# Four weights' low parts on GpSimd, and the first Fourier stage of the second tokens in half-sized steps

## The chip, the cores and the metric

The kernel runs on one core of one Trainium2 chip. The metric is device time in microseconds (us) for one execution. The core's engines work side by side, each through its own queue in order: TensorE (PE, with its weight loads as PEld), VectorE (DVE), ScalarE (ACT), GpSimd (POOL), and SyncE (SP), which here only issues DMAs. ScalarE and GpSimd issue DMAs too. An engine waits where an instruction needs something that another engine or a DMA has not delivered, and whatever stands behind it in that queue waits with it.

## The reference

Both branches start from the layer-normalized input, and their sum is added to the input:

```python
xn = _layernorm(x)                      # x: 1 x 2048 x 448
# A: a state-space filter, as a convolution by FFT of length 4096
K = 2.0 * einsum("dn,dnl->dl", C, exp(A * dt * pos)).real
y = irfft(rfft(xn) * rfft(K))[:2048] + xn * D_skip
# B: a gated unit with 1792 inner features
h = sigmoid(xn @ w_gate) * (xn @ w_up)
out = x + y + h @ w_down
```

## The kernel before

The kernel is written in two generators, `conv()` for branch A and `glu()` for branch B. A driver at the end of the kernel steps them alternately, by estimated cost, so that the program has their instructions interleaved. The compiler's scheduler then fixes one order for each engine from the order of the program, from priorities, and from a model of when each instruction could start; instructions inside `hp(HP)` count as if they stood 300 places earlier. On the chip this order does not change. Tiles come from pools: a tile's tag has a fixed number of buffers (`bufs`), and a new tile waits until an older one of that tag is done with.

**Branch B.** The 2048 tokens are worked on in two halves of 1024, each in two groups `t` of 512. The 1792 features are 14 blocks `f` of 128, in five groups (3, 3, 3, 3, 2 blocks). A weight is kept as the sum of a rounded high part and a low part, so that each product is three matmuls: high by high, low by high, high by low. In the first half of the tokens, for each `f` (lines 741 to 764): the raw weights are loaded into `wraw` (one buffer, by SyncE), ScalarE rounds them to `wh` (line 748), VectorE subtracts to get `wl` (line 752; for the very first weight line 750), and for some `f` both are stored for the second half. In the second half some weights are loaded raw again and split on GpSimd (lines 757 to 759). `gate(w, xs, ...)` for a pair (f, t) then issues two groups of 11 matmuls (line 698), each into one PSUM bank of the tag `gu` (four buffers); ScalarE takes the tanh of the first bank (L706), VectorE multiplies by the second into `hf` (L709), ScalarE rounds it to `hh` (L714) and VectorE makes `hl` (L716). Both have six buffers. After all blocks of a group, the down matmuls go into `po` (line 811, also tag `gu`), and VectorE adds them to `acc` (L816). The down weights' low parts `dl` are made on GpSimd (L775).

**Branch A.** `prep` turns the filter's parameters into tables, in long runs of VectorE operations with single ScalarE steps (lines 336 to 417); its low parts are subtractions on GpSimd (L393). It runs while the first two groups of branch B do. `kgen` then makes the filter in 56 chunks: GpSimd the magnitudes (L503), PE the phases into `tr` (L526), ScalarE the sines `S` (L535 to L538), VectorE the products `Et` and `Ft` (L589 to L591), PE the sums `ko` (L603). `spectra` multiplies the spectra and transforms back, in the last quarter.

**The first Fourier stage** of the input (`x_first_stage`, line 281) makes four pieces g of each pair of token blocks, each by two matmuls into one bank. For blocks 0 to 7 `x_spec` does it. For blocks 8 to 15 it is put into the last feature group of the first half (`cross`, f = 12 and 13), whose gates run in the order (12, 0), (13, 0), (12, 1), (13, 1). There each pair of blocks b = 8, 10, 12, 14 goes through four steps: `pair_load` brings its tokens into two tiles with the tags `hh` and `hl`; `pair_norm` normalizes them; `pair_turn` transposes them for branch B's second half; and `pair_first` does the Fourier stage: it takes four `gu` banks, issues eight matmuls into them (sixteen rows of the profile, which shows each of these float32 matmuls as two), and copies each bank to an `x1` tile (two pieces in the single `wraw` buffer, two in the two `rd` buffers), from which ScalarE's queue issues two DMAs each. Three tables say where the steps stand: `mid[n]` between the two matmul groups of the n-th gate, `end[n]` behind that gate, `downs[t, b]` behind the down matmuls of group t and block b.

Of the kernel before, what the change touches and what calls it, by code (L numbers as in the profile page):

```python
# [32 lines left out]
WS = 4.5  # L33
WP = 5
WX = 2
HELD = 12.6
HP = 300
Y0 = (8, 1)
# [92 lines left out]
def s4d_glu_kernel(ctx, tc, io):  # L131
# [142 lines left out]
    def row(b, g):  # L274
        return 32 * (b // 4 % 2) + 8 * g + 4 * (b // 8) + b % 4
# [391 lines left out]
        with hp(HP):  # L667
            x_transpose(xns, xq[-1], 128 * (b % 4))

    def pair_first(b, xns):  # L670

        x1 = pg.tile([128, 2, D], F32, name="x1", tag="wraw", bufs=1)
        pss = [psg.tile([128, 512], F32, name="gu", bufs=4) for _ in range(4)]
        for g in range(4):
            x_first_stage(pss[g][:, :D], xns, g)
        for g in range(4):
            to = x1[:, g] if g < 2 else pg.tile([128, D], F32, name="x1", tag="rd", bufs=RB)
            nc.scalar.copy(to, pss[g][:, :D])
            for i in range(2):
                nc.scalar.dma_start(x1_d[:, row(b + i, g)], to[64 * i : 64 * i + 64])  # L680

    def gate(w, xs, to, between=None, behind=False):
        wh, wl = w
# [35 lines left out]
    def glu():  # L719
        for half in range(2):  # L720
# [4 lines left out]
            for fs_ in ORDER[half]:  # L725
# [8 lines left out]
                if cross:  # L734
                    xts = {b: pair_load(b) for b in range(8, 16, 2)}
                    step = lambda f_, b: f_(b, xts[b])
                    mid = [(pair_norm, 8), None, (pair_first, 8), (pair_first, 10)]
                    end = [(), ((pair_turn, 8), (pair_norm, 10)), ((pair_turn, 10), (pair_norm, 12)), ((pair_turn, 12), (pair_norm, 14))]
                    downs = {(0, 0): (pair_first, 12), (0, 1): (pair_turn, 14), (0, 3): (pair_first, 14)}
                for n_, (f, t) in enumerate(order):  # L740
                    if t == 0:
                        wh = pg.tile([128, 2, 4, 128], F32R, name="wh", bufs=2)
                        if half == 0:
                            first = len(raws) == 2
                            raw, rd = raws.pop() if raws else (w_load(f), None)
                            wl = w_low()
                            with hp(HP):
                                nc.scalar.copy(wh, raw)
                                if first:
                                    v.scalar_tensor_tensor(wl, raw, lim[:, 0, 0:1], wh, ALU.mult, ALU.subtract)  # L750
                                else:
                                    v.tensor_tensor(wl, raw, wh, ALU.subtract)  # L752
                            if f not in RAW:
                                for t_, d_ in kept((wh, wl), wt_d, f):
                                    nc.sync.dma_start(d_, t_)
                        elif f in RAW:
                            raw, wl = w_load(f, eng=nc.gpsimd), w_low()
                            nc.gpsimd.tensor_copy(wh, raw)
                            nc.gpsimd.tensor_tensor(wl, raw, wh, ALU.subtract)
                        else:  # L760
                            wl = w_low()
                            for t_, d_ in kept((wh, wl), wt_d, f):
                                nc.sync.dma_start(t_, d_)
                        ws.append((wh, wl))
                    between = (lambda s_=mid[n_]: step(*s_)) if cross and mid[n_] else None

                    yield from gate(ws[f - f0], xq[2 * half + t], hs[t], between, half == 0 and (f, t) == (1, 0))
                    if t == 0:
                        dh = pg.tile([128, D], F32R, name="dh", bufs=FCH[0])
                        if half == 0:  # L770
                            rd = rd or rd_load(f)
                            dl = d_low()
                            with hp(HP), tc.issue_after((act if f == 1 else marks)[0].ins):
                                nc.scalar.copy(dh, rd)
                            nc.gpsimd.tensor_tensor(dl, rd, dh, ALU.subtract)  # L775
                            if f not in RAW:
                                for t_, d_ in kept((dh, dl), dt_d, f):
                                    nc.sync.dma_start(d_, t_)
                        elif f in RAW:
                            dl = d_low()  # L780
                            rd = rd_load(f, pg.tile([128, D], F32, name="rdw", tag="wraw", bufs=1), nc.gpsimd)
                            nc.gpsimd.tensor_copy(dh, rd)
                            nc.gpsimd.tensor_tensor(dl, rd, dh, ALU.subtract)
                        else:
                            dl = d_low()
                            for t_, d_ in kept((dh, dl), dt_d, f):
                                nc.sync.dma_start(t_, d_)
                        wts.append((dh, dl))
                    yield 1.25
                    for s_ in end[n_] if cross else ():  # L790
                        step(*s_)
                    if cross:
                        yield 2
                for t in range(2):
                    acc = accs[2 * half + t]
                    for b in range(4):
                        if final and (t, b) == (0, 1):

                            yield None
                        if final and (t, b) == (1, 2):  # L800

                            sp_mm[:] = glu_mm
                            for m in (0, 2):
                                lasts[0](1, m)
                        po = psg.tile([128, D], F32, name="po", tag="gu", bufs=4)
                        bs = slice(128 * b, 128 * b + 128)
                        n = 0
                        with tc.issue_after(sp_mm[0].ins) if glu_on else nullcontext():
                            for (hh, hl), (dh, dl) in zip(hs[t], wts):
                                for a_, w_ in ((hh, dh), (hh, dl), (hl, dh)):  # L810
                                    glu_mm[:] = [nc.tensor.matmul(  # L811
                                        po, a_[:, bs], w_, start=(n == 0), stop=(n == 3 * fc - 1)
                                    )]
                                    n += 1
                        with hp(HP):
                            v.scalar_tensor_tensor(  # L816
                                acc[:, b], po, 0.5, acc[:, b], ALU.mult, ALU.add
                            )
                        yield 0.6 * fc
                        if cross and (t, b) in downs:  # L820
                            step(*downs[t, b])
                    if cross:
                        nc.sync.dma_start(acc_d[:, 4 * t : 4 * t + 4], acc)
                    if final:
# [332 lines left out]
```

## Time and profile before

| | us |
|---|---|
| runs, median of 3 | 745.98 |
| runs, lowest and highest | 745.71, 748.92 |
| the profiled execution, its own time | 749.33 |
| its span, first to last instruction | 747.5 |
| PE busy in the span | 700.4 |
| DVE, ACT, POOL busy | 561.7, 424.8, 346.7 |

The mean granted TensorE clock was 0.982. PE's first matmul starts at 12.06 us. Rows of the timeline have the start in us, the length in us, the engine, the line, the operation, output and inputs with their shapes, the count of merged instructions, and in brackets the idle time before them with what ended it. A "q" behind an engine's name is its sequencer, which issues DMAs and waits. A row of a window has its stretch and length, then the busy time (and count of instructions) of PE, PEld, DVE, ACT and POOL, the granted clock, the DMA engines' share and GB/s. Successive matmuls overlap, so the lengths of single ones add up to more than the time they take together.

### The profile page before, as it was taken

To read this page: it belongs to the slowest core of one execution; us is meant where nothing else is said; L and a number is where in the kernel's file an instruction comes from. 1 tells how busy PE (TensorE), PEld (TensorE's weight loads), DVE (VectorE), ACT (ScalarE), POOL (GpSimd) and SP (SyncE) were. 2 spreads that over 40 slices of the span, in tenths; PEclk is the share of its full clock that TensorE was granted. 3 is DMA by queue.
4 is the path that set the end of the run, shared out by engine and by line. 5 is a ranking of instruction groups with operands and counts; after the bars stand their busy time and mean duration, and the time that the engine had idled before them with its cause. 6 is when DMAs were issued, how large, how long until landed. Compare 5 with 4: busy or idle time off the path is not lost.

```text
span 747.5 us, 19396 instructions
## 1 busy us (share of the span) xinstructions
PE 700.4 (94%) x7892; PEld 551.6 (74%) x7892; DVE 561.7 (75%) x776; ACT 424.8 (57%) x651; POOL 346.7 (46%) x423
## 2 busy tenths in 40 slices
PE   3997989998999989899999999999999999999995
PEld 2774868877778778566878887887877777776784
DVE  6899997698879889768778977977864655465533
ACT  3543865677668767697677687767653222323320
POOL 2110036884855966826565586486743200441002
PEclk9998999999999999899999999999999999999998
DMA  9964356253115443365842332232157999999746
GB/s 208 233 186 141 87 171 203 83 179 126 43 52 183 150 118 114 100 182 160 273 140 68 108 93 69 93 96 68 43 159 216 293 249 247 262 253 234 187 107 165
DMA packets 98952, 114.75 MB, mean 154 GB/s; under 512 B 11888, under 2 KB 86832, under 8 KB 98864
## 3 DMA queue, kind: packets, MB, share of 16 engines
q1 hardware_dynamic: 74704, 89.11, 43.5%
q10 hardware_dynamic: 21584, 18.24, 9.0%
q0 software_dynamic: 2576, 6.17, 3.1%
q8 instruction: 62, 1.02, 0.6%
q14 instruction: 26, 0.21, 0.1%
HBM read 69.64 MB, written 43.84 MB: 152 GB/s over the span
## 4 chain that ended last, share of the span: by engine, by line
PE 60%; DMA 13%; DVE 11%; ACT 7%; SPq 4%; issue 4%; ACTq 0%; POOL 0%; DVEq 0%; POOLq 0%
PE gu L698 22%; PE po L811 14%; PE tr L526 6%; PE ko L603 6%; PE sp L893 4%; DMA sx<-x_d 3%; PE pv L920 3%; DMA tb<-in_c_tab_dram 2%; DVE Ft L591 1%; DMA wraw<-in_B_w_gate_dram 1%; ACT S L538 1%; PE kp L553 1%; DMA xe<-in_A_u_dram 1%; DVE Et L589 1%; DVE wl L752 1%
## 5 line engine op out<-in xcount | busy, mean ns | idle before, releaser
L503 POOL TENSOR_TENSOR me<-me,pm 128x32 f32<-128x32 f32 (+1 forms) x168 | 134.0, 797 | 135.2 <-DVE Et L590 122.7
L503 POOL TENSOR_TENSOR mf<-mf,pm 128x64 f32<-128x64 f32 (+1 forms) x112 | 113.9, 1017 | 4.3
L698 PE MATMUL gu<-xh,wh 128*128 128x512 f32 x336 | 98.5, 402 | 5.2 <-DVE hf L709 5.2
L698 PE MATMUL gu<-xh,wl 128*128 128x512 f32 x336 | 100.1, 396 | 0.0
L698 PE MATMUL gu<-xl,wh 128*128 128x512 f32 x336 | 95.9, 391 | 0.0
L589 DVE TENSOR_TENSOR Et<-me,S 128x1024 f32<-128x1024 f32 x56 | 83.3, 1487 | 15.6 <-ACT S L538 15.4
L590 DVE TENSOR_TENSOR Et<-me,S 128x1024 f32<-128x1024 f32 x56 | 74.9, 1338 | 24.4 <-ACT me L516 17.2
L811 PE MATMUL po<-dh,hh 128*128 128x448 f32 x224 | 84.9, 379 | 2.8 <-DVE acc L816 2.1
L811 PE MATMUL po<-dl,hh 128*128 128x448 f32 x224 | 83.0, 371 | 0.0
L811 PE MATMUL po<-dh,hl 128*128 128x448 f32 x224 | 82.8, 371 | 0.0
L535 ACT ACTIVATE S<-tr 128x1024 f32<-128x1024 f32 x56 | 57.5, 1027 | 43.3 <-PE tr L526 41.1
L698 PEld LDWEIGHTS gu<-xh,wh 128*128 128x128 f32 x336 | 62.4, 191 | 23.5 <-DVE hf L709 6.2
L591 DVE TENSOR_TENSOR Ft<-mf,S 128x1024 f32<-128x1024 f32 x56 | 77.7, 1387 | 1.2 <-ACT S L538 0.7
L603 PEld LDWEIGHTS ko<-Et,Ft 128*32 128x32 f32 x3584 | 54.6, 111 | 30.7 <-DVE Ft L591 10.5
L698 PEld LDWEIGHTS gu<-xh,wl 128*128 128x128 f32 x336 | 63.3, 189 | 18.1 <-issue 4.1
L603 PE MATMUL ko<-Et,Ft 128*32 128x64 f32 x3584 | 64.8, 223 | 12.0 <-DVE Ft L591 8.8
L698 PEld LDWEIGHTS gu<-xl,wh 128*128 128x128 f32 x336 | 62.9, 188 | 13.6
L714 ACT CAST hh<-hf 128x512 fp32r<-128x512 f32 x56 | 34.8, 621 | 63.4 <-DVE hf L709 61.1
L526 PE MATMUL tr<-sel,ph 128*128 128x512 f32 x224 | 66.1, 417 | 0.7 <-ACT S L537 0.5
L538 ACT ACTIVATE S<-S,hpi 128x1024 f32<-128x1024 f32 x56 | 65.4, 1168 | 1.2 <-DMA dt_d<-dl 1.2
L816 DVE SCALAR_TENSOR_TENSOR acc<-po,acc 128x448 f32<-128x448 f32 x80 | 47.8, 611 | 22.2 <-PE po L811 22.2
L709 DVE SCALAR_TENSOR_TENSOR hf<-th,gu 128x512 f32<-128x512 f32 x56 | 38.1, 680 | 31.4 <-PE gu L698 27.9
(199 smaller groups left out, 1301.9 us busy)
## 6 DMA issues: line engine op xcount, KB each, us to landing
sk_d<-sk ACTq DMA_DIRECT2D x14, 512.0 KB
sx<-x_d SPq DMA_DIRECT2D x32, 224.0 KB
skl<-sk_d SPq DMA_DIRECT2D x16, 448.0 KB
vp<-v_d SPq DMA_DIRECT2D x16, 448.0 KB
v_d<-vt SPq DMA_DIRECT2D x62, 112.0 KB
wt_d<-wh SPq DMA_DIRECT2D x9, 512.0 KB
wt_d<-wl SPq DMA_DIRECT2D x9, 512.0 KB
wl<-wt_d SPq DMA_DIRECT2D x9, 512.0 KB
```

The source lines that it names most:

```text
L503: ins = nc.gpsimd.tensor_tensor(m[:, :, w + a : 2 * w : n], m[:, :, a:w:n], par(base + i).unsqueeze(2).to_broadcast([128, 4 * DC, w // n]) ...
L526: nc.tensor.matmul(ps[:, h], ph[:, cn % 2, 128 * h : 128 * h + 128], sel[:, i], start=(i == 0), stop=(i == 1),)
L535: nc.scalar.activation(rows(cs), pv, AF.Abs)
L538: sins[:] = [nc.scalar.activation(cs, cs, AF.Sin, scale=-TWO_PI, bias=hpi)]
L589: v.tensor_tensor(Et[:, :, :, 32:64], two(me[:, :, 32:64]), S[:, 1::-1], ALU.mult)
L590: v.tensor_tensor(Et[:, :, :, 0:32], two(me[:, :, 0:32]), S[:, 1:3, :, ::-1], ALU.mult)
L591: fts[:] = [v.tensor_tensor(Ft, two(mf), S[:, 3:5], ALU.mult)]
L603: mm = nc.tensor.matmul(ko[32 * j : 32 * j + 32, sl], Ft[:, cc, DC * h + 4 * q + j], Et[:, cc, DC * h + 4 * q + j], start=(k == 0), stop=( ...
L698: glu_mm[:] = [nc.tensor.matmul(ps, a_, b_, start=(n == 0), stop=(n == len(mm) - 1))]
L709: marks[1] = v.scalar_tensor_tensor(hf, th, 1.0, pgu[1], ALU.add, ALU.mult)
L811: glu_mm[:] = [nc.tensor.matmul(po, a_[:, bs], w_, start=(n == 0), stop=(n == 3 * fc - 1))]
L816: v.scalar_tensor_tensor(acc[:, b], po, 0.5, acc[:, b], ALU.mult, ALU.add)
```

## The change

Two edits. First, for f in `EARLY`, that is 2, 3, 4 and 5, the subtraction that makes `wl` in the first half is issued on GpSimd instead of VectorE. All others stay.

Second, `pair_first` is replaced by `pair_half(b, xns, p)`, which does the pieces 2p and 2p + 1 alone: two `gu` banks, four matmuls (eight rows of the profile), two copies and four DMAs. `pair_low` is p = 0, with its `x1` tile in the `wraw` buffer; `pair_high` is p = 1, with its two in the `rd` buffers. In the tables, `pair_low` stands where `pair_first` stood for blocks 8, 10 and 12; `pair_high` of 8 and of 10 stands in `end[2]` and `end[3]`, behind the same gate as its low half and behind the `pair_turn` and `pair_norm` of the next pairs; `pair_high` of 12 follows `pair_turn` of 14; and the pair of 14 has its low half at `downs[0, 2]` and its high half at `downs[0, 3]`.

```diff
+EARLY = range(2, 6)
...
-    def pair_first(b, xns):
-
-        x1 = pg.tile([128, 2, D], F32, name="x1", tag="wraw", bufs=1)
-        pss = [psg.tile([128, 512], F32, name="gu", bufs=4) for _ in range(4)]
-        for g in range(4):
-            x_first_stage(pss[g][:, :D], xns, g)
-        for g in range(4):
-            to = x1[:, g] if g < 2 else pg.tile([128, D], F32, name="x1", tag="rd", bufs=RB)
+    def pair_half(b, xns, p):
+
+
+        x1 = None if p else pg.tile([128, 2, D], F32, name="x1", tag="wraw", bufs=1)
+        pss = [psg.tile([128, 512], F32, name="gu", bufs=4) for _ in range(2)]
+        for g in range(2):
+            x_first_stage(pss[g][:, :D], xns, 2 * p + g)
+        for g in range(2):
+            to = pg.tile([128, D], F32, name="x1", tag="rd", bufs=RB) if p else x1[:, g]
             nc.scalar.copy(to, pss[g][:, :D])
             for i in range(2):
-                nc.scalar.dma_start(x1_d[:, row(b + i, g)], to[64 * i : 64 * i + 64])
+                nc.scalar.dma_start(x1_d[:, row(b + i, 2 * p + g)], to[64 * i : 64 * i + 64])
+
+    def pair_low(b, xns):
+        pair_half(b, xns, 0)
+
+    def pair_high(b, xns):
+        pair_half(b, xns, 1)
...
-                    mid = [(pair_norm, 8), None, (pair_first, 8), (pair_first, 10)]
-                    end = [(), ((pair_turn, 8), (pair_norm, 10)), ((pair_turn, 10), (pair_norm, 12)), ((pair_turn, 12), (pair_norm, 14))]
-                    downs = {(0, 0): (pair_first, 12), (0, 1): (pair_turn, 14), (0, 3): (pair_first, 14)}
+                    mid = [(pair_norm, 8), None, (pair_low, 8), (pair_low, 10)]
+                    end = [
+                        (),
+                        ((pair_turn, 8), (pair_norm, 10)),
+                        ((pair_turn, 10), (pair_norm, 12), (pair_high, 8)),
+                        ((pair_turn, 12), (pair_norm, 14), (pair_high, 10)),
+                    ]
+                    downs = {
+                        (0, 0): ((pair_low, 12),), (0, 1): ((pair_turn, 14), (pair_high, 12)),
+                        (0, 2): ((pair_low, 14),), (0, 3): ((pair_high, 14),),
+                    }
...
-                                    v.tensor_tensor(wl, raw, wh, ALU.subtract)
+                                    (nc.gpsimd if f in EARLY else v).tensor_tensor(wl, raw, wh, ALU.subtract)
...
-                            step(*downs[t, b])
+                            for s_ in downs[t, b]:
+                                step(*s_)
```

## The prediction

> **What bounds the kernel now.** The engine totals of the page first, then four stretches of the span (busy us of each engine, count of instructions, granted TensorE clock, DMA share, GB/s).
>
> ```profile
> PE 700.4 (94%) x7892; PEld 551.6 (74%) x7892; DVE 561.7 (75%) x776; ACT 424.8 (57%) x651; POOL 346.7 (46%) x423
> ...
> core 0: us, PE busy (x) PEld busy (x) DVE busy (x) ACT busy (x) POOL busy (x), PEclk, DMA share, GB/s
> 40.00:115.00 75.00, 65.21 (x312) 48.04 (x310) 73.58 (x122) 41.19 (x69) 13.36 (x9) 0.95 0.51 149
> 120.00:300.00 180.00, 170.52 (x2225) 140.97 (x2224) 152.35 (x166) 128.03 (x184) 124.57 (x143) 0.98 0.39 122
> 300.00:360.00 60.00, 56.35 (x789) 37.55 (x787) 46.96 (x59) 45.44 (x76) 36.20 (x50) 0.94 0.55 153
> 360.00:555.00 195.00, 194.74 (x2875) 160.50 (x2869) 156.90 (x162) 138.77 (x196) 121.39 (x145) 1.00 0.35 107
> ```
>
> TensorE (PE) sets the pace: from 360 to 555 it stands still for 0.26 us of 195, so what is won or lost earlier is carried to the end one for one. Both edits act where it does stand still. From 40 to 115 it idles 9.79 us while VectorE (DVE) is busy 73.58 of 75: there VectorE is the bound. From 300 to 360 it idles 3.65 us. The timeline of PE names what ended the longer spells (in brackets: idle before, releaser), and windows around them show the clock.
>
> ```profile
> 68.69 0.74 PE L811 MATMUL po<-dh,hh 128*128 128x448 f32 x1 [2.13 <-DVE acc L816]
> 100.34 0.98 PE L698 MATMUL gu<-xh,wh 128*128 128x512 f32 x3 [1.98 <-DVE hf L709]
> 189.96 0.75 PE L603 MATMUL ko<-Et,Ft 128*32 128x64 f32 x38 [1.84 <-DVE Ft L591]
> 304.72 0.99 PE L281 MATMUL gu<-xt,wx 32*64 32x448 f32 x12
> 308.20 1.94 PE L603 MATMUL ko<-Et,Ft 128*32 128x64 f32 x64 [2.49 <-DVE Et L589]
> 310.07 1.76 PE L281 MATMUL gu<-xt,wx 32*64 32x448 f32 x4
> ```
>
> ```profile
> 65.30:72.10 6.80, 4.67 (x17) 2.81 (x9) 6.80 (x10) 0.91 (x1) 0.00 (x0) 0.50 0.65 195
> 98.30:103.00 4.70, 2.72 (x12) 2.13 (x12) 4.70 (x10) 3.79 (x8) 1.03 (x1) 1.00 0.54 158
> 191.60:195.00 3.40, 3.40 (x10) 2.91 (x9) 2.90 (x3) 2.28 (x3) 3.32 (x3) 0.50 0.58 158
> 307.70:314.40 6.70, 6.20 (x74) 4.14 (x75) 5.07 (x5) 2.56 (x5) 4.17 (x7) 0.50 0.46 103
> ```
>
> A spell of 2.13, 1.84 or 2.49 us stands before or in a stretch of 6.80, 3.40 or 6.70 us at half clock; the one of 1.98 us kept 1.00. So about 2 us of idling is where half clock begins, and it costs half of PE's work in the stretch: 3.10 us of the 6.20 in the last row.
>
> **Part 1: `wl` of f = 2 to 5 on GpSimd (POOL).** Removed from VectorE: four subtractions. Added to POOL: the same four, plus their way through its queue. ScalarE's copies to `wh` that release them, then the subtractions, in the timeline; below them the price of the form on each engine (min/median/max).
>
> ```profile
> 38.39 1.05 ACT L748 CAST wh<-wraw 128x1024 fp32r<-128x1024 f32 x1
> 59.85 1.05 ACT L748 CAST wh<-wraw 128x1024 fp32r<-128x1024 f32 x1 [4.95 <-DMA wraw<-in_B_w_up_dram]
> 91.36 1.04 ACT L748 CAST wh<-wraw 128x1024 fp32r<-128x1024 f32 x1
> ...
> 39.48 1.23 DVE L752 TENSOR_TENSOR wl<-wraw,wh 128x1024 fp32r<-128x1024 f32 x1 [0.65 <-ACT wh L748]
> 48.87 1.22 DVE L752 TENSOR_TENSOR wl<-wraw,wh 128x1024 fp32r<-128x1024 f32 x1
> 63.86 1.21 DVE L752 TENSOR_TENSOR wl<-wraw,wh 128x1024 fp32r<-128x1024 f32 x1
> 96.67 1.21 DVE L752 TENSOR_TENSOR wl<-wraw,wh 128x1024 fp32r<-128x1024 f32 x1
> ...
> L759 POOL TENSOR_TENSOR wl<-wraw,wh x5: 2354/2387/2394, 536.8 to 670.0; 128x1024 fp32r<-128x1024 f32 x5
> ```
>
> VectorE gives up 1.23 + 1.22 + 1.21 + 1.21 = 4.87 us of work. Whether it gains them depends on what POOL's 2.39 us do to it. These rows put the same operation with and without a POOL subtraction running:
>
> ```profile
> 104.12 1.68 POOL L393 TENSOR_TENSOR aim<-aim,p 112x512 fp32r<-112x512 f32 x1 [0.83 <-DVE fr L400]
> 107.09 1.61 POOL L393 TENSOR_TENSOR aim<-aim,p 112x512 fp32r<-112x512 f32 x1 [1.29 <-ACT GG L428]
> ...
> 101.34 0.68 DVE L398 SCALAR_TENSOR_TENSOR w<-aim,w 112x512 f32<-112x512 f32 x1
> 104.57 1.78 DVE L398 SCALAR_TENSOR_TENSOR w<-aim,w 112x512 f32<-112x512 f32 x1
> 107.48 0.67 DVE L709 SCALAR_TENSOR_TENSOR hf<-th,gu 128x512 f32<-128x512 f32 x1
> ```
>
> L398 alone takes 0.68. Started at 104.57 under POOL's 104.12 to 105.80, it ends at 106.35, 0.55 after POOL: it was held until POOL was done. L709, which reads one operand from PSUM, takes 0.67 right under another POOL subtraction. So a POOL subtraction holds VectorE's SBUF operations for its whole length. For f = 3, 4 and 5 VectorE, without a pause there, gives up 1.2 and is held 2.39: 1.2 us lost each. For f = 2 it idled 0.65 before the subtraction anyway: 2.39 - 1.23 - 0.65 = 0.5 lost. Together +4.1 us, and since PE's spells at 68.69 and 100.34 are ended by VectorE, PE comes out of this stretch later by as much.
>
> What else hangs on these four. PE's first use of the f = 2 low part, and what stands on POOL and SyncE (SP) at f = 3:
>
> ```profile
> 42.26 0.96 PE L698 MATMUL gu<-xh,wl 128*128 128x512 f32 x3
> ...
> 49.33 1.79 POOL L775 TENSOR_TENSOR dl<-rd,dh 128x448 fp32r<-128x448 f32 x1 [11.77 <-ACT dh L774]
> ...
> 51.14 0.35 SPq L637 DMA_DIRECT2D rd<-in_B_w_down_dram  x1
> 52.13 0.38 SPq L629 DMA_DIRECT2D wraw<-in_B_w_gate_dram  x1
> ```
>
> For f = 2 POOL ends at 39.44 + 2.39 = 41.83, 0.4 before PE wants it; with that cover gone PE would wait for the rest. For f = 3 the `wl` now stands ahead of or behind this `dl`; SP's `rd` load waits for that `dl` and the next raw weights stand behind it, so they come about 1.2 later, and ScalarE, which already waits 4.95 us for them at 59.85, holds its queue as much longer. That lateness runs beside VectorE's, so nothing is added. For f = 4 and 5 POOL is free when `wh` ends (60.90 and 92.40), so `wl` ends at 63.3 and 94.8 instead of 65.07 and 97.88 and `wraw` comes free earlier: the next loads land sooner, which no spell above waits for.
>
> The clock: the spell of 1.98 us grows past 2.13, so I add one stretch of 3.40 at half clock, 1.7 us. Value for part 1: 4.1 + 1.7 = +5.8. Ends: -4.9 if POOL holds nothing back, and 4 x 2.39 - 4.87 + 2 x 1.7 = +8.1 with no idle time used and two such stretches. I stand near the upper end, since the rows of the hold are in this very stretch.
>
> **Part 2: first Fourier stage in halves.** Matmuls, copies and DMA issues stay as many; their places change. `pair_first` took all four `gu` banks at once. For tokens 8 that is the sequence of rows at 304.72: twelve matmuls for three banks, then 64 `ko` matmuls that wait for VectorE until 308.20, then the last four, and only behind these the second group of the gate of f = 12. With `pair_low` eight matmuls (as the profile counts them) take two banks, and the gate's group finds its bank where the third was free before. PE's price of a gate, from the chain of waits, and what VectorE and ScalarE did then:
>
> ```profile
> 440.64 5.01 PE gu L698 x22
> ...
> 304.72 2.08 DVE L591 TENSOR_TENSOR Ft<-mf,S 128x1024 f32<-128x1024 f32 x1
> 306.72 1.43 DVE L589 TENSOR_TENSOR Et<-me,S 128x1024 f32<-128x1024 f32 x1
> ...
> 316.92 0.59 ACT L218 CAST xh<-gu 128x512 fp32r<-128x512 f32 x1 [4.46 <-PE gu L212]
> 317.53 0.62 ACT L714 CAST hh<-hf 128x512 fp32r<-128x512 f32 x1
> ...
> L680 ACTq DMA_DIRECT2D x_d<-x x32: 452/532/1194, 307.9 to 355.0; - x32
> ```
>
> Eleven gate matmuls are 2.5 us. Four first-stage matmuls fewer start the spell 0.3 earlier: 2.49 + 0.3 - 2.5 leaves 0.3 of it, 2.2 won, and with so short a spell the 3.10 of half clock too: -5.3. The high half then issues eight matmuls (0.66), two copies and four DMAs (0.53 each) per pair behind the transposes and the normalization of the next pairs; ScalarE's queue gets no more of them than before. Ends: 0 if the order of PE's queue keeps the `ko` matmuls ahead of the gate, -5.3 if not, +8.9 by the last rival. I take -5.3, because the bank was what stood between the gate and PE.
>
> By the Trainium skill (TensorE: Matmul & The Clock Gate, Part 1) the clock drops to half after an idle window of about 3.4 us. No spell here is so long, yet the rows show 0.50 after 1.84 us, so the trace disagrees; by the page the two clock terms would fall away and the sum would be 746.0 + 4.1 - 2.2 = 747.9.
>
> **The sum.** 5.8 - 5.3 = +0.5. The profiled execution took 749.33 us (747.5 of span and 1.8 around it), which makes 749.8; it stands 3.35 above the median of the runs, so on that median of 745.98 the forecast is 746.5: no change.
>
> **The rivals.**
> Gap stays: the `ko` matmuls keep their place before the gate, because PE's order is fixed when the kernel is built and VectorE's rows above (2.08, with POOL holding it) stay as slow. Part 2 brings nothing: 746.0 + 5.8 = 751.8. Against it: one bank less is asked for.
> Relief: half of POOL's time falls on VectorE work it can't hold, as L709 shows, or on idle time, and VectorE's order lets the results PE waits for come first. Part 1 is then worth nothing: 746.0 - 5.3 = 740.7 (with all of its gain, 735.8). Against it: VectorE's 73.58 of 75. The Trainium skill (SBUF — State Buffer, Who interferes with whom) has an operation with at most one SBUF input outside the two-port modes never held, and one with two held for the whole GpSimd instruction; the trace agrees for L709 and L398.
> Slots, on the slow side: the `hh` and `hl` slots number six; four hold the pairs' tokens, two the first results of f = 12 and 13. So `hh` of (12, 1) waits until a pair is done, now for `pair_high` of tokens 8, which stands behind that gate, a transposition and a normalization. If its eight matmuls end after `hf`, ScalarE waits at L714 with all that feeds the filter's chunks behind it. I price such a stall like the 4.46 at 316.92, twice (tokens 8 and 10): 746.5 + 8.9 = 755.4. It decides from stalls of 3.3 us in all (slower by over 0.5%). Against it: eight matmuls are 0.66 us.
>
> **How the numbers follow.** Forecast 0.32, gap stays 0.26, relief 0.31, slots 0.11. A measurement of this kernel tells about 0.5% (3.7 us) from no change. Faster: 0.30 of relief and 0.03 of the forecast, 0.33. Slower: 0.24 of gap stays, 0.11 of slots, 0.05 of the forecast, 0.40. Same: 0.27. The forecast's own range is 742 to 750; over the cases 738 to 756 leaves out the full gain of part 1 and the worst of slots.
>
> **What would show it.** Part 1: four `wl` rows of about 2.4 us on POOL before 100 us, VectorE's SBUF operations beside them longer by as much, PE's idle time from 40 to 115 above 9.79. Less idle there means relief. Part 2: no `ko` wait of over 1 us behind the first eight L281 matmuls, and no half clock near 307; a wait there means gap stays. `hh` L714 waiting on L281 means slots. The prediction is wrong if VectorE's order of work differs so much that the spells of PE move elsewhere.

## The result and the profile after

| | before | after |
|---|---|---|
| median (lowest to highest), us | 746.38 (745.63 to 748.92), 6 runs | 755.9 (751.95 to 761.12), 6 runs |
| profiled execution, its own time | 749.33 | 755.62 |
| its span | 747.5 | 753.5 |
| PE busy | 700.4 | 706.5 |
| span less PE busy | 47.1 | 47.0 |

The changed kernel is slower: ratio 1.013 [1.0087, 1.0173]. In two later comparisons, with 12 runs each, the ratio was 1.0096 [1.0059, 1.0134] and 1.0093 [1.0055, 1.0131]. The forecast was 746.5. Ratios and their intervals here and below leave out the few slow runs, which the medians in the tables contain, so a ratio is not the quotient of two medians.

The last two rows of the table already say where to look. PE's idle time is the same to 0.1 us, and its busy time has grown by 6.1 us, though it has the same 7892 matmuls. First the engine totals from the page of the changed kernel, then its windows: the stretches that the prediction shows of the kernel before, and one more. The columns are the same.

```profile
PE 706.5 (94%) x7892; PEld 553.7 (73%) x7892; DVE 559.6 (74%) x772; ACT 423.0 (56%) x650; POOL 363.3 (48%) x427
```

```profile
40.00:115.00 75.00, 66.00 (x305) 48.80 (x304) 74.41 (x118) 40.40 (x70) 32.63 (x13) 0.93 0.50 143
120.00:300.00 180.00, 169.21 (x2227) 139.89 (x2225) 149.19 (x164) 125.58 (x179) 120.22 (x142) 0.99 0.38 119
300.00:360.00 60.00, 57.11 (x649) 35.46 (x649) 42.22 (x49) 44.35 (x74) 33.04 (x41) 0.89 0.47 136
360.00:555.00 195.00, 194.75 (x2871) 160.39 (x2870) 159.06 (x169) 137.55 (x197) 125.60 (x154) 1.00 0.37 110
344.00:357.60 13.60, 13.60 (x44) 6.26 (x43) 5.64 (x8) 6.36 (x9) 3.04 (x6) 0.50 0.26 59
```

From 40 to 115, where part 1 acts, PE idles 9.00 us and idled 9.79 before. From 300 to 360, where part 2 acts, PE is busy for 0.76 us more and yet does 140 matmuls fewer (649 for 789), with VectorE 4.7 us less busy (the changed kernel is some 3 us behind by then, so the two stretches don't hold quite the same work). The last row is new: 13.60 us without a moment's idling, all of it at half clock. Grouped by line, from 295 to 362, the first-stage matmuls of the second tokens (columns: count | busy us, mean ns | idle before, releaser); the fences are before, after, and part 1 alone (experiment e1, which has them in the order of before):

```profile
L281 PE MATMUL gu<-xt,wx 32*64 32x448 f32 x64 | 9.7, 586 | 0.0
```

```profile
L282 PE MATMUL gu<-xt,wx 32*64 32x448 f32 x64 | 15.2, 648 | 2.0 <-DVE xr L226 2.0
```

```profile
L282 PE MATMUL gu<-xt,wx 32*64 32x448 f32 x64 | 8.9, 560 | 0.0
```

The same 64 rows take 15.2 us instead of 9.7: 5.5 of the 6.1 us. Two things are in these 5.5. At full clock the rows of the changed order take 12.3 us (e5 and e16 below) and those of the order of before 8.9 (e1): 3.4 us. The other 2.1 are half clock. PE's timeline of the changed kernel shows both.

```profile
307.54 0.98 PE L282 MATMUL gu<-xt,wx 32*64 32x448 f32 x8
308.45 0.96 PE L706 MATMUL gu<-xh,wh 128*128 128x512 f32 x3
...
341.04 1.62 PE L282 MATMUL gu<-xt,wx 32*64 32x448 f32 x8 [2.04 <-DVE xr L226]
...
346.09 1.75 PE L282 MATMUL gu<-xt,wx 32*64 32x448 f32 x2
...
348.33 1.75 PE L282 MATMUL gu<-xt,wx 32*64 32x448 f32 x2
...
350.58 1.76 PE L282 MATMUL gu<-xt,wx 32*64 32x448 f32 x4
...
356.51 1.51 PE L282 MATMUL gu<-xt,wx 32*64 32x448 f32 x8
```

Read the counts against the lengths. Two rows take 1.75 us at half clock, and so do four (1.76). At full clock eight take 0.98, and twelve took 0.99 in the kernel before. First-stage matmuls that stand directly behind each other run side by side; each uses only 32 rows and 64 columns of the array. A float32 matmul is two rows: in the trace the first rows of neighbours start 7 ns apart, and so do the second rows, 0.43 us behind. What costs is not the matmul but the *burst*, a set of such rows with nothing between them: 0.96 to 0.99 us at full clock, however many rows it has up to twelve. (A burst whose rows come in two lots is longer, as the 1.62 at 341.04.) The kernel before has 9 bursts, the changed kernel 12.

The Trainium skill (TensorE: Matmul & The Clock Gate, Part 3: Packing small matmuls — row/col tiling) says so: matmuls at different tile positions run concurrently, and a pack takes one matmul's duration plus about 4 ns for each further tile. The trace agrees that they run side by side; here the starts lie 7 ns apart, not 4.

The gap near 305 did close: eight rows at 307.54, and the gate follows at 308.45. In its place stands the 2.04 at 341.04. It is `pair_high` of tokens 12, which waits for VectorE. From about 344, some 3 us behind that wait, the clock is at half until 357.6, and four bursts lie in that stretch. VectorE's timeline there:

```profile
336.93 2.04 DVE L592 TENSOR_TENSOR Ft<-mf,S 128x1024 f32<-128x1024 f32 x1 [1.54 <-POOL mf L504]
338.89 1.64 DVE L591 TENSOR_TENSOR Et<-me,S 128x1024 f32<-128x1024 f32 x1
340.56 0.42 DVE L226 TENSOR_TENSOR xr<-gu,xr 64x256 fp32r<-64x256 f32 x1
```

`xr` reads the bank in which the transposes of `pair_turn` of 14 stand, and frees it. In VectorE's queue it is behind the filter's `Ft` and `Et`. The change put `pair_high` of 12 behind that `pair_turn`, so it asks for just that bank.

One profile is one execution, though. Summed over windows of 2 us, PE's busy time multiplied by the part of the clock that was not granted is 8.8 us before and 13.5 after, an estimate by which 4.7 of the 6.0 us between these two spans are clock. PE's busy time without this is 1.5 us more (693.1 for 691.6), in e2, e5 and e16 2.0 to 2.5 more: below the 3.4 of the rows, in part because the end of a burst overlaps the next matmul (0.98 long at 307.54, the next at 308.45). Another profile of the same changed kernel (e5) has no half clock from 300 to 360 and was longer still, 757.09 us, with 51.8 us of PE's idling in place of 47.0. Profiles tell here where time can go; how much the change costs, the medians tell.

Part 1 on GpSimd (POOL), then on VectorE:

```profile
40.29 2.42 POOL L768 TENSOR_TENSOR wl<-wraw,wh 128x1024 fp32r<-128x1024 f32 x1 [1.83 <-ACT wh L764]
49.49 5.39 POOL L768 TENSOR_TENSOR wl<-wraw,wh 128x1024 fp32r<-128x1024 f32 x1 [6.78 <-ACT wh L764]
54.85 1.57 POOL L791 TENSOR_TENSOR dl<-rd,dh 128x448 fp32r<-128x448 f32 x1
64.55 4.98 POOL L768 TENSOR_TENSOR wl<-wraw,wh 128x1024 fp32r<-128x1024 f32 x1 [8.13 <-ACT wh L764]
...
94.67 6.10 POOL L768 TENSOR_TENSOR wl<-wraw,wh 128x1024 fp32r<-128x1024 f32 x1 [7.23 <-ACT wh L764]
```

```profile
40.25 0.17 DVE L257 TENSOR_SCALAR ve<-mv 128x8 f32<-128x8 f32 x1
40.45 2.29 DVE L258 TENSOR_SCALAR ys<-ve 128x8 int32<-128x8 int32 x1
...
52.52 0.68 DVE L717 SCALAR_TENSOR_TENSOR hf<-th,gu 128x512 f32<-128x512 f32 x1
53.12 4.46 DVE L312 SCALAR_TENSOR_TENSOR pl<-pl,fr 112x514 f32<-112x514 f32 x3
...
67.21 0.62 DVE L832 SCALAR_TENSOR_TENSOR acc<-po,acc 128x448 f32<-128x448 f32 x1
...
98.45 0.67 DVE L717 SCALAR_TENSOR_TENSOR hf<-th,gu 128x512 f32<-128x512 f32 x1
99.05 2.15 DVE L415 TENSOR_SCALAR a<-a,ex 112x256 f32<-112x256 f32 x2
```

Only the first `wl` takes the 2.4 us of the form; the others take 5.39, 4.98 and 6.10. The rows fit a POOL that is held, from its start until VectorE comes to an operation that reads PSUM. For f = 3 that is `hf` at 52.52, and 2.36 us later, at 54.88, `wl` ends; for f = 4 it is `acc` at 67.21, and `wl` ends at 69.53, 2.32 later; for f = 5 it is `hf` at 98.45, and `wl` ends at 100.77, 2.32 later. While it runs at last, it holds the next VectorE operation. L258 takes 2.29 in place of 0.17 (2.1 more), the first L312 2.32 in place of 0.69 (1.6 more), the first L415 1.88 in place of 0.34 (1.5 more). For f = 4 the timeline shows no VectorE operation that is longer.

### The profile page after: what moved, and what is told of

Same layout as the page of the kernel before. It is cut to its first block, busy times and chain, and to the rows that moved or that the text cites. A ratio compares the mean times of both kernels' runs of the same rounds, so it can differ in the third digit from the quotient of the medians.

```text
span 753.5 us, 19395 instructions
## 1 busy us (share of the span) xinstructions
PE 706.5 (94%) x7892; PEld 553.7 (73%) x7892; DVE 559.6 (74%) x772; ACT 423.0 (56%) x650; POOL 363.3 (48%) x427
## 4 chain that ended last, share of the span: by engine, by line
PE 68%; DVE 11%; DMA 8%; ACT 4%; issue 3%; POOL 2%; SPq 2%; ACTq 0%; DVEq 0%; POOLq 0%
PE gu L706 28%; PE po L827 13%; PE sp L910 7%; PE ko L604 6%; PE tr L527 6%; PE pv L937 4%; PE gu L282 1%; DVE Et L591 1%; DVE Ft L592 1%; DVE pl L312 1%; DMA sx<-x_d 1%; PE kp L554 1%; DMA xe<-in_A_u_dram 1%; DVE Et L590 1%; DMA wraw<-in_B_w_gate_dram 1%
## 5 line engine op out<-in xcount | busy, mean ns | idle before, releaser
L504 POOL TENSOR_TENSOR mf<-mf,pm 128x64 f32<-128x64 f32 (+1 forms) x112 | 109.9, 981 | 4.2
L722 ACT CAST hh<-hf 128x512 fp32r<-128x512 f32 x56 | 34.8, 622 | 60.0 <-DVE hf L717 60.0
```

The costliest lines, as they stand in the source:

```text
L504: ins = nc.gpsimd.tensor_tensor(m[:, :, w + a : 2 * w : n], m[:, :, a:w:n], par(base + i).unsqueeze(2).to_broadcast([128, 4 * DC, w // n]) ...
```

## The experiments

Each kernel was run beside the kernel before on the same chip, kernels of one group together. Part 1 and the halves of the pairs 8, 10 and of 12, 14 can be put in by themselves, which gives the first two groups.

| run | part 1 | halves 8, 10 | halves 12, 14 | median | before | ratio [95%] |
|---|---|---|---|---|---|---|
| e1 | yes | | | 750.65 | 749.72 | 0.9992 [0.996, 1.0024] |
| e2 | | yes | yes | 751.0 | 749.72 | 1.0031 [0.9994, 1.0068] |
| e3 | | yes | | 747.17 | 749.72 | 0.9962 [0.9933, 0.9992] |
| e4 | | | yes | 754.33 | 749.72 | 1.0052 [1.0021, 1.0084] |
| e5 | yes | yes | yes | 755.18 | 747.53 | 1.0096 [1.0059, 1.0134] |
| e6 | yes | yes | | 747.53 | 747.53 | 1.0005 [0.9976, 1.0034] |
| e7 | yes | | yes | 752.9 | 747.53 | 1.0069 [1.0035, 1.0103] |
| e8 | yes | yes | yes, high 12 ahead | 749.53 | 747.53 | 1.0046 [1.0017, 1.0075] |
| e9 | yes | yes, kept together | yes, kept together | 785.74 | 748.95 | 1.0496 [1.0454, 1.0539] |
| e10 | | yes, kept together | whole, kept together | 786.69 | 748.95 | 1.0513 [1.0475, 1.0552] |
| e11 | | whole, kept together | whole, kept together | 771.44 | 748.95 | 1.0329 [1.0285, 1.0374] |
| e12 | | whole, scattered | whole, scattered | 756.09 | 748.95 | 1.0117 [1.0077, 1.0158] |
| e13 | | yes | | 748.11 | 748.27 | 1.0009 [0.9978, 1.004] |
| e14 | f = 4 alone | yes | | 751.38 | 748.27 | 1.0054 [1.0023, 1.0085] |
| e15 | f = 3 alone | yes | | 747.65 | 748.27 | 1.0003 [0.9967, 1.0038] |
| e16 | | yes | yes | 752.65 | 747.85 | 1.0063 [1.0029, 1.0096] |
| e17 | yes | yes | yes | 755.94 | 747.85 | 1.0093 [1.0055, 1.0131] |

**The parts alone: e1 to e4.** e1 is the kernel before with part 1, e2 the changed kernel with `EARLY = ()`. In e3 the pairs 12 and 14, in e4 the pairs 8 and 10 keep their whole step (`pair_first` is put back beside the half steps):

```diff
 e3, against e2
-                        (0, 0): ((pair_low, 12),), (0, 1): ((pair_turn, 14), (pair_high, 12)),
-                        (0, 2): ((pair_low, 14),), (0, 3): ((pair_high, 14),),
+                        (0, 0): ((pair_first, 12),), (0, 1): ((pair_turn, 14),),
+                        (0, 3): ((pair_first, 14),),
 e4, against e2
-                    mid = [(pair_norm, 8), None, (pair_low, 8), (pair_low, 10)]
+                    mid = [(pair_norm, 8), None, (pair_first, 8), (pair_first, 10)]
...
-                        ((pair_turn, 10), (pair_norm, 12), (pair_high, 8)),
-                        ((pair_turn, 12), (pair_norm, 14), (pair_high, 10)),
+                        ((pair_turn, 10), (pair_norm, 12)),
+                        ((pair_turn, 12), (pair_norm, 14)),
```

> The first edit alone (wl of f = 2 to 5 on GpSimd), pair_first as before. Theory: in the changed kernel GpSimd's four subtractions took 2.4, 5.4, 5.0 and 6.1 us because VectorE's back-to-back SBUF operations kept it out, so results behind them (dl of f = 3, the raw weights of f = 4) came 3 to 5 us late; PE was 3.4 us behind at the gate of f = 6. So about 749 us, the gate of f = 6 starting 3 us later than before. Rival, all of the loss is in the second edit: 746. Rival, all of it is in the first: 755.

> The second edit alone (all four pairs in halves), wl on VectorE as before. Theory: the wait near 305 goes and PE is about 5 us ahead by the end of the gate (13, 1), then a wait of 2 us for xr at pair_high of 12 and 13.65 us at half clock take back more than that: 749 to 752, with half clock between 335 and 360. Rival, the second edit only gains: 741. Rival, all of the loss is here: 755.

> Halves for the pairs 8 and 10 alone; 12 and 14 by pair_first as before, wl on VectorE. Theory: the gain near 305 stays and the loss behind 335 does not come: 741 to 742, no half clock from 300 to 360. Rival, half clock there is a matter of where the windows of the clock fall and not of pairs 12 and 14: 746 or more, half clock of some 7 us somewhere from 300 to 360.

> Halves for the pairs 12 and 14 alone; 8 and 10 by pair_first as before, wl on VectorE. Theory: the wait of 2.5 us near 305 with its half clock stays, and the wait for xr with half clock behind 335 comes on top: 751 to 755. Rival, the halves of 12 and 14 cost nothing by themselves: 746.

These texts count from 746, while the kernel before took 749.72 beside these four, so the ratios are what compares. Part 1 alone can't be told from no change. The halves of 8 and 10 alone came out a little below before, those of 12 and 14 above: what the prediction had counted as a gain is worth little, and the late pairs, which it had not priced, cost.

They don't cost in the way that the expectation of e4 has it. Its profile has no wait for `xr`: `pair_high` of 12 waits 0.46 us, for `acc`. Nor is it bursts alone: e4 has 10 of them and L282 is busy 10.6 us, e7 below has 9 and 10.2, at most 1.7 above the 8.9 of e1. What these two have more of is idling of PE, 51.4 and 53.0 us in the span (before 47.1, e1 49.2). Some of it lies behind the first stage; in e4:

```profile
374.28 1.10 PE L604 MATMUL ko<-Et,Ft 128*32 128x64 f32 x64 [0.85 <-DVE Ft L592]
...
382.59 1.10 PE L604 MATMUL ko<-Et,Ft 128*32 128x64 f32 x64 [1.08 <-DVE Ft L592]
```

Why VectorE is late there was not settled.

**Two by two: e5 to e7.** e6 is e3, e7 is e4, each with `EARLY = range(2, 6)`.

> The whole change once more, beside the same runs of the kernel before as the three kernels that go with it. Separate theory: the parts act independently, so the ratio to before is the product of part 1 alone (0.9992) and part 2 alone (1.0031), 1.0023 +- 0.004, about +1.7 us; the 1.013 of the first comparison then held some 7 us that belong to its few runs. Rival, joint theory: part 1 moves VectorE's and TensorE's work so that the wait of 2.04 us for xr draws a long stretch at half clock behind it; the ratio is again 1.010 to 1.016 and the profile shows over 10 us at half clock between 335 and 360.

> Part 1 and the halves of the pairs 8 and 10; the pairs 12 and 14 are done whole. Separate theory: 0.9992 x 0.9962 = 0.9954, about -3.4 us, no wait of TensorE over 1.5 us between 300 and 360. Joint theory of part 1 with the early pairs: what part 1 delays falls on the pairs 8 and 10 too, 1.003 or more. If this is near 0.995 and the whole change near 1.013, the loss needs the pairs 12 and 14.

> Part 1 and the halves of the pairs 12 and 14; the pairs 8 and 10 are done whole. Separate theory: 0.9992 x 1.0052 = 1.0044, about +3.3 us. Joint theory of part 1 with the late pairs: 1.010 or more, with a stretch of over 6 us at half clock between 330 and 360.

The late pairs cost with and without part 1: e4 against the mean of e3 and e13 0.66%, e7 against e6 0.64%. e5 and e7 lie between the two theories, with intervals that touch both, and the interval of e6 leaves out 0.9954 and takes in 1.003, though the 0.9954 was built on the gain of e3, which did not come back (e13). The profile of e5 has none of the half clock between 335 and 360 that the joint theory asks for.

**The place of one step: e8.**

```diff
-                        (0, 0): ((pair_low, 12),), (0, 1): ((pair_turn, 14), (pair_high, 12)),
+                        (0, 0): ((pair_low, 12),), (0, 1): ((pair_high, 12), (pair_turn, 14)),
```

> The whole change with one edit: behind the down matmuls (0, 1) pair_high of 12 comes ahead of pair_turn of 14 instead of behind it. Theory of the wait for xr (the high half of 12 takes banks that are freed only by VectorE's xr, which stands behind Ft and Et in its queue): the first stage L282 of that half no longer waits 2.04 us for xr, and with the wait goes the half clock behind it; 3 to 7 us below e5_whole. Rival: the late pairs cost because their halves cut TensorE's and ScalarE's queues into more pieces, wherever they stand; within 2 us of e5_whole. Second rival: the wait moves to the transposes of pair_turn of 14, which then find the banks taken: same time as e5_whole, with a wait of 1.5 to 2.5 us at L213 instead of L282.

e8 is 5.65 us below e5 in the medians, within what the first theory gave (by the ratios 0.50%, 3.7 us, and the intervals overlap). PE's timeline of e8:

```profile
338.64 0.98 PE L282 MATMUL gu<-xt,wx 32*64 32x448 f32 x8
...
340.85 1.09 PE L213 MATMUL gu<-ident,xt 128*128 128x128 f32 x6 [1.23 <-DVE xr L226]
...
343.10 1.10 PE L604 MATMUL ko<-Et,Ft 128*32 128x64 f32 x64 [1.15 <-DVE Et L590]
```

The half step no longer waits. But the second rival has a part in it: the transposes now wait 1.23 for the same `xr`, and the `ko` matmuls 1.15, in sum no less than the 1.49 and 0.63 of e5. What else e8 has less of is bursts. The group of L282 by line, for e5 and for e8:

```profile
L282 PE MATMUL gu<-xt,wx 32*64 32x448 f32 x64 | 12.3, 560 | 1.5 <-DVE xr L226 1.5
```

```profile
L282 PE MATMUL gu<-xt,wx 32*64 32x448 f32 x64 | 10.7, 560 | 0.0
```

Neither profile has half clock in these rows: 12 bursts take 12.3 us, and 11 in e8 take 10.7. The 1.6 between them is one burst less and one that is not broken in two by a wait. That is 1.6 of some 4 to 6 us; the rest the two profiles don't place. This group led to the theory of bursts, which none of the expectations so far had.

**Bursts: e9 to e12.** In e12 nothing but the priority of the first-stage matmuls is changed in the kernel before, which makes the scheduler put them into 16 places of PE's order instead of 9. In e9 to e11 a block keeps the matmuls of each step together (shown for e11; the same in `pair_half` for e9, and in both for e10).

```diff
 e12
-        for g in range(4):
-            x_first_stage(pss[g][:, :D], xns, g)
+        with hp(HP):
+            for g in range(4):
+                x_first_stage(pss[g][:, :D], xns, g)
 e11
-        for g in range(4):
-            x_first_stage(pss[g][:, :D], xns, g)
+        with tc.tile_critical():
+            for g in range(4):
+                x_first_stage(pss[g][:, :D], xns, g)
```

> The whole change, with the matmuls of each half step of the first Fourier stage kept together in TensorE's order. Burst theory: matmuls of this stage that stand directly behind each other run side by side, so that a burst takes about 0.97 us whether it has 2, 4, 8 or 12 rows; the whole change has 12 bursts of them (the kernel before 9), here there are 8. Four bursts fewer are 3.9 us: ratio about 1.0096 - 0.0052 = 1.004, and L282 is busy about 8 us instead of 12.3 at full clock. Rival, waits: the loss of the whole change is the wait for xr and what follows it; glued bursts wait for both banks at once, so nothing is won: 1.008 to 1.012.

> The halves of the pairs 8 and 10 alone, the pairs 12 and 14 whole, each step's first-stage matmuls kept together: 6 bursts instead of 10. Burst theory: 3.9 us less than that kernel had without it (ratio 0.9962), so about 0.991, L282 busy about 6.5 us instead of 10.7. Rival, waits: a whole pair has to wait until four banks are free, TensorE's idle time between 325 and 360 grows by 2 to 4 us, and the ratio is 0.996 or more.

> The kernel before with the eight first-stage matmuls of each pair kept together: 4 bursts instead of 9. Burst theory: 5 x 0.97 = 4.9 us less, ratio about 0.9935, L281 busy about 4.5 us instead of 8.9 at full clock. Rival, waits: four banks free at once come late, the spell near 305 grows beyond 2.5 us with half clock behind it, and the ratio is 1.000 or more.

> The kernel before with the first-stage matmuls of each pair at high priority: nothing else is edited, every pair is done whole, but TensorE's order then has them in 16 bursts instead of 9. Burst theory: 7 x 0.97 = 6.8 us more, ratio about 1.009, L281 busy about 15.5 us at full clock. Rival, waits: the stage comes no later than before and no bank is asked for sooner by a new step, so the time stays within 0.3% of before, unless TensorE's idle time between 300 and 360 grows by as much.

e12 came out where the burst theory put it: 1.0117 for 1.009, and the 0.3% of its rival lies outside the interval. (The profiled execution, 761.78 us, is the longest of its eleven; half clock is in one of its bursts, as in the kernel before.) Its rows by line, four of its bursts, and its window:

```profile
L281 PE MATMUL gu<-xt,wx 32*64 32x448 f32 x64 | 16.3, 586 | 0.0
```

```profile
302.55 0.97 PE L281 MATMUL gu<-xt,wx 32*64 32x448 f32 x4
303.45 0.31 PE L603 MATMUL ko<-Et,Ft 128*32 128x64 f32 x4
303.68 0.96 PE L281 MATMUL gu<-xt,wx 32*64 32x448 f32 x2
304.57 0.41 PE L212 MATMUL gu<-ident,xt 128*64 128x128 f32 x2
304.91 0.96 PE L281 MATMUL gu<-xt,wx 32*64 32x448 f32 x2
305.80 0.54 PE L603 MATMUL ko<-Et,Ft 128*32 128x64 f32 x24
306.28 0.97 PE L281 MATMUL gu<-xt,wx 32*64 32x448 f32 x4
```

```profile
300.00:360.00 60.00, 58.72 (x711) 35.12 (x709) 44.03 (x54) 46.84 (x78) 35.41 (x44) 0.94 0.43 122
```

PE idles 1.28 us in this window, where before it idled 3.65. Behind it, from 360 to 555, it idles 2.71 in place of 0.26, so over both windows it waits as long as before (3.99 and 3.91), and is slower all the same. Twelve rows that took 0.99 us in one burst take 3.86 in four. No half step and no part 1 is in this kernel, and no more matmuls.

e9 to e11 failed as tests of fewer bursts. A kept-together block waits for more than its banks: in e9 the first one stands 5.82 us for GpSimd's `mf`, which its matmuls don't read, and the bursts behind such waits run at half clock.

```profile
313.18 1.76 PE L282 MATMUL gu<-xt,wx 32*64 32x448 f32 x7 [5.82 <-POOL mf L504]
```

```profile
311.00 1.80 PE L281 MATMUL gu<-xt,wx 32*64 32x448 f32 x16 [2.12 <-POOL mf L503]
```

The second fence is e11: all sixteen rows of a pair in one burst of 1.80 us at half clock, no longer than the two rows of the changed kernel (1.75). That bears out the price of a burst. Whether fewer bursts without such waits would gain, as the price says (1 us each), was not settled.

**One weight at a time: e13 to e15.** e13 is e3 again; e14 and e15 add `EARLY = (4,)` and `EARLY = (3,)`.

> The kernel of e3_halves_8_10 once more, as the base of the next two and because it came out below the kernel before (0.9962, upper bound 0.9992). If that holds: 0.993 to 0.999. If it was chance: 0.999 to 1.002.

> The halves of the pairs 8 and 10, and wl of f = 4 alone on GpSimd. Hold theory of the prediction: VectorE is held for the 2.39 us of the subtraction and freed of 1.21, +1.2 us against e13. Starved theory: GpSimd's subtraction waits for VectorE, runs where VectorE reads PSUM and then holds at most one SBUF operation; for f = 4 it held none in the whole change, so VectorE gains 1.2 and the raw weights come later: within 1 us of e13. In the profile: wl of f = 4 takes 4 to 6 us on GpSimd, and no VectorE operation beside it is longer by over 0.5 us.

> The halves of the pairs 8 and 10, and wl of f = 3 alone on GpSimd. Hold theory: the same +1.2 us as for f = 4. Starved theory: wl takes about 5.4 us, holds a VectorE SBUF operation for about 2 us when it runs at last, and dl of f = 3 behind it in GpSimd's queue ends 5 us later than without; TensorE waits 1 us or more for dl and hl at the down matmuls near 56, which it doesn't in e14. About +1 to +2 us against e13.

The small gain of e3 did not come back: the two ratios are 0.9962 and 1.0009, their mean 0.9986. Both theories of e14 and e15 missed the times. The row of `wl` did what the starved theory said (4.13 us in e14, first fence), but the cost in e14 came 100 us later, on PE (second) and on VectorE (third):

```profile
62.70 4.13 POOL L780 TENSOR_TENSOR wl<-wraw,wh 128x1024 fp32r<-128x1024 f32 x1 [10.92 <-ACT wh L776]
```

```profile
171.77 1.45 PE L604 MATMUL ko<-Et,Ft 128*32 128x64 f32 x64 [4.56 <-DVE Ft L592]
```

```profile
168.76 1.23 DVE L780 TENSOR_TENSOR wl<-wraw,wh 128x1024 fp32r<-128x1024 f32 x1 [7.69 <-DMA rd<-in_B_w_down_dram]
...
170.50 1.22 DVE L592 TENSOR_TENSOR Ft<-mf,S 128x1024 f32<-128x1024 f32 x1
```

A later weight comes late here, its `wl` stands ahead of `Ft` on VectorE, and PE waits 4.56 us. On VectorE the order is the same in e13, where that `wl` starts at 161.63 and `Ft` at 163.43. What differs is SyncE's queue. In e14 it has a store of `dl` ahead of the second half of that weight:

```profile
162.10 0.32 SPq L806 DMA_DIRECT2D dt_d<-dl  x1
...
164.56 0.40 SPq L630 DMA_DIRECT2D wraw<-in_B_w_up_dram  x1
```

The store goes out only when GpSimd has made `dl` (160.48 to 162.08). In e13 the load stands ahead of that store, at 151.81, and the store follows at 158.91. So the scheduler had drawn up another order after the edit, and PE's new wait is about the +3.3 us of e14 over e13. The time of one subtraction is less than what a new fixed order can add or save elsewhere.

**The whole beside part 2: e16 and e17.**

> Part 2 alone once more, on the same chip and beside the same runs of before as e17. If the two parts only add up: 1.000 to 1.006, as e2_part2 had it.

> The whole change beside part 2 alone. Separate theory: part 1 adds what it adds without part 2, between -3 and +2 us (ratio of part 1 alone 0.9992, its interval 0.996 to 1.0024), so e17 is at most 2 us above e16. Joint theory: part 1 costs only where the halves are too; e17 is 3 to 7 us above e16, ratio to before 1.008 to 1.013.

3.3 us between the medians and 0.30% (2.2 us) between the ratios: between the two theories. Over the four pairs of kernels with and without part 1 (e1 to before, e6 to the mean of e3 and e13, e7 to e4, e17 to e16) the ratios differ by -0.08, +0.19, +0.17 and +0.30%, on average +0.15%, about 1 us, with intervals too wide to tell it from nothing. Part 2 alone has 1.0031 and 1.0063, on average 0.47% or 3.5 us. The two together are 4.6 us; the whole was 7.0 and 7.2 us above before in the later comparisons. Some of the rest is clock. Over the 123 runs of the kernel before that the ratios use, 0.01 less of the mean granted clock goes with 5.3 us more. The runs of e5 and e17 had 0.0056 and 0.0042 less than those of before beside them (e16 0.0039), which by this estimate is 3.0 and 2.2 us; 4.2 and 4.8 us are left. Why the clock is lower in them on average, the runs don't show.

Half clock after the wait for `xr` came back in e17, behind a wait of 2.08 us:

```profile
346.70:360.20 13.50, 13.50 (x44) 6.23 (x43) 5.64 (x8) 6.33 (x9) 3.04 (x6) 0.50 0.27 59
```

In e2 there is none behind a wait of 2.04, and in e5 and e16 none behind waits of 1.49 and 1.50.

## Why the prediction was wrong, by its steps

**What bounds the kernel.** Right in the main. In the profile after, PE idles 0.25 us from 360 to 555, as before, and what was lost earlier is in the end time; in other profiles it idles more there (1.64 us in e5, 2.75 in e4).

**Part 2, -5.3: this is the step that failed.** Measured, part 2 alone is +3.5 us (e2 and e16). The sentence "Matmuls, copies and DMA issues stay as many; their places change" took the cost of PE's work as fixed, and priced the eight matmuls of a half at 0.66 us, as a share of a longer burst. The same share is in the sum: four matmuls fewer were to start the wait 0.3 us earlier, but eight rows take 0.98 and twelve 0.99. The runs show a price by burst, 0.97 us each (e12: seven more bursts, +1.17%). Three bursts more, one of them in two lots, make 12.3 us of first stage (e5, e16) where the order of before takes 8.9 (e1): +3.4 us. The row that shows it stood in the prediction's own fence: 12 rows in 0.99 us, and then 4 rows in 1.76 at half clock. The prediction also gave the wait near 305 a whole 5.3. It did go, together with its half clock, as foretold. But e1, with the order of before in this stretch, has there a wait of 1.53 and no half clock, so in some executions there is less to win. In e3 and e13 the halves of 8 and 10, for which the whole -5.3 was reckoned, gave 0.9986 on average: 1 us, after 1.8 us more of first stage (10.7 for 8.9), and not told from nothing.

**The pairs 12 and 14** were not in the sum at all; the prediction's working followed tokens 8. That put them at nothing, and they cost 0.64 and 0.66% (e7, e4), nearly 5 us. How they cost is shown only in part. Where all four pairs are in halves, `pair_high` of 12 behind `pair_turn` of 14 made a new wait of 1.5 to 2.1 us for `xr`. In two of five profiles (the changed kernel and e17, not e2, e5 and e16) about 13.5 us of half clock came behind it, and four of the twelve bursts fell into that: 15.2 us instead of 12.3. e8 shows that the place of that one step matters. But e4 and e7 cost as much without this wait and with hardly more bursts, by more idling of PE, part of it other waits for VectorE, and why it came stays open.

**Part 1, +5.8: right in the stretch, too large in size.** The hold of 2.39 us each was read from one row, L398, and laid on each whole subtraction. In fact POOL waits for VectorE, begins beside an operation that reads PSUM, and makes VectorE's operations longer by 2.1 + 1.6 + 0 + 1.5 = 5.2 us, against the 4.87 that VectorE gave up: +0.3 instead of +4.1. (Only the first `wl`, for f = 2, began at once.) What PE loses, as far as the trace shows, comes through lateness. `wl` of f = 3 took 5.39 us, `dl` behind it came late, and PE's timeline of the changed kernel has

```profile
56.47 0.47 PE L827 MATMUL po<-dl,hh 128*128 128x448 f32 x1 [1.31 <-POOL dl L791]
56.78 0.37 PE L827 MATMUL po<-dh,hh 128*128 128x448 f32 x1
58.23 0.47 PE L827 MATMUL po<-dh,hl 128*128 128x448 f32 x1 [1.08 <-DVE hl L724]
```

The prediction saw this `dl` and took it to be hidden. PE's idle time from 40 to 115 did not rise above 9.79. Measured, part 1 costs about 1 us, which can't be told from nothing. The profiles put it somewhat higher: PE comes to the first stage at 304.6 to 310.2 us, on average 307.0, in the seven with the whole of part 1 (the changed kernel, e1, e5 to e8, e17), and at 302.9 to 305.8, on average 304.4, in the six without (before, e2, e3, e4, e13, e16).

**The rivals.** "Gap stays" fell: the gate took the freed place at 308.45. "Relief" had the right mechanism for part 1, half of POOL's time on work that it can't hold, but no gain came of it, since VectorE still lost as much as it gave up and results came late. "Slots" gave 755.4, almost the measured time, for a reason that did not occur: in the changed kernel ScalarE's copies to `hh` (L722) near 304 and 320 follow other work at once, and PE's new wait is for VectorE's `xr`. The measured 755.9 lies at the upper edge of the range of 738 to 756, which the slots rival had stretched that far; that the range held it is luck.

**The clock.** The prediction's "about 2 us of idling is where half clock begins" is too firm as a rule: among its rows half clock came behind 1.84 and not behind 1.98, and the stretch from 65.30 had begun before the spell of 2.13, which lasts from 66.56 to 68.69. In the later runs 2.04 and 2.08 were followed by 13.6 and 13.5 us of it, another 2.04 (e2) by none.

## What to carry to other kernels

Before you cut a step into smaller ones, look at whether its matmuls run side by side: compare the lengths of rows with different counts, and price PE's part by the number of separate bursts, not by the number of matmuls. Look for the rows that free the buffer that a moved step asks for, on the queue where they stand, for each moved step and not only the first. And with an order fixed when the kernel is built, an edit worth 1 us can be outweighed by what the new order does 100 us later (4.56 in e14), so an edit of that size is judged by runs and not by a sum.

## What the runs showed of the hardware that was not expected

- Bursts of 2, 4, 8 and 12 rows on 32 by 64 parts of the array take 0.96, 0.97, 0.98 and 0.99 us.
- Half clock can last while PE is busy without a break: 13.60 of 13.60 us at 0.50 in the changed kernel, 13.50 of 13.50 in e17. PEld is busy only 6.26 and 6.23 of it, and first-stage bursts are 6.8 of the 13.6 (1.75 + 1.75 + 1.76 + 1.51). By the Trainium skill (TensorE: Matmul & The Clock Gate, Part 1) a busy window of about 3.4 us brings full clock back. The trace disagrees if busy means that matmuls run; what the chip counts instead no run here shows.
- Beside VectorE's operations on SBUF, one right behind the other, a GpSimd subtraction of 2.4 us took 2.6 to 3.7 us more (5.39, 4.98, 6.10), and ended 2.32 to 2.36 us after the start of a VectorE operation that reads PSUM.
- Over 123 runs of the kernel before, 0.01 less of the mean granted clock went with 5.3 us more of some 748.
